# Turning the state with 64x64 products, and joining the inverse straight after X, in an RWKV-7 kernel with a GELU MLP

## The chip, the cores and the metric

The kernel runs on one core of a Trainium2 chip. The time is device time in microseconds of one execution. A core has five engines that run at the same time and each take their own instructions in order: TensorE (PE in the profile) multiplies matrices[...], ScalarE (ACT) evaluates functions and copies, VectorE (DVE) and GpSimd (POOL) work element by element, and SyncE (SP) issues most of the DMA transfers. An engine waits on semaphores until what it reads has been written and what it overwrites has been read.

## The reference

Inputs r, k, v, w, a, b have the shape (4 batches, 8 heads, 768 steps, 40). Each head keeps a 40x40 state:

```
y[t]   = r[t] . state
Sa     = state . a[t]
state  = state * w[t]  -  outer(Sa, b[t])  +  outer(v[t], k[t])
```

The y of all heads are put side by side to x (3072 x 320), and then

```
h = x @ w_in            # 320 x 2048
out = gelu(h) @ w_out   # 2048 x 320, exact (erf) GELU
```

## The kernel before

**Chunks.** The 768 steps are cut into 12 chunks of 64 steps. Inside a chunk the recurrence becomes matrix products; the state passes from chunk to chunk. Everything is float32. The 32 pairs of batch and head are laid in halves of 64 partitions: tiles are written [P, e, i, g, d] or the like, where e and x stand for halves, i counts pairs of heads, and g pairs of batches. Most products are therefore 64x64, 40x64 or 32x32 blocks, four or more of which have different places in TensorE's array (`mm`, line 100). `units` lists the 64 places (g, i, x, e).

**A turn of the loop** for chunk c (n = c+1, n2 = c+2 are the chunks that are prepared ahead) issues, in this order for TensorE: `corner` (J, 64 products of 32x32, and the copy Js on ScalarE), `make_X` (X, the state times a, summed with avs on VectorE), a piece of the MLP, `joined` (J again, 64 products of 32x32 from Js and the fetched T2 and Tt; then half of the result is copied to Tt by ScalarE and half by VectorE, line 723), a piece of the MLP, `make_sa` and `make_saT` from Tt and X, an MLP piece, `make_y2` (from the turned state) and `make_M`, an MLP piece, `make_QY`, `outputs` (y, and the new state, on VectorE), an MLP piece, `make_A(n)`, `sums(n2)`, `turn_state`, `make_av(n)`, an MLP piece, `make_RV(n)`, `make_N(n2)`, and two more MLP pieces. The order on each engine is the order in which the program issues (`manual_schedule`); there is no planner that moves it.

**The MLP** of a finished chunk is a generator of eight pieces; `fill()` runs the next one. Four pieces are `ph` (line 914, 40 products with w_in each, then Gelu on ScalarE, line 916), and from chunk 3 on the other four are `po` of `seven` (line 867, products with w_out in a scheme with seven products in place of eight; its sums on VectorE are lines 852, 871, 881, 887, 888 and 919). In `seven` the stores of the output are issued on SP; a `ph` piece issues no DMA.

**sums(n2)** makes the running products of the decays. TensorE writes the sums of log w to two PSUM tiles: wT_ps, turned, and cum, in rows. ScalarE then takes exponentials (line 436): wp = exp(+wT_ps), en = exp(-wT_ps), each in two instructions, one for each g, and rw = exp(-cum) (line 438; its tile is named part in the profile). wp scales a (`scale_a`, line 498, VectorE) and the new state, en scales the turned b and k (lines 507 and 525, VectorE), and rw scales the rows of b (`scale_b`, line 476, VectorE) and of k (`scale_k`, line 483, POOL).

**turn_state** transposes the state for `make_y2` of the next chunk: `flip` (line 446) makes eight 128x128 transposes on TensorE into the PSUM tile tn_ps, and ScalarE copies them to the tile turned (line 836).

**The inverse.** Each chunk needs the inverse of a triangular 64x64 matrix for each head. `make_N(n2)` makes N on TensorE, VectorE masks it (line 562), SP stores it to DRAM (line 599) and loads it as Nb in another layout (line 648). POOL inverts 32x32 blocks column by column (`start_inverse`, lines 656 and 658, 62 instructions with `scale_k` among them), and issues the store itself (line 670). In the next turn SP fetches the result as Tt and T2 (`fetch_inverse`, lines 680 and 684), VectorE turns a part of it to L (`turn_corner`, line 693), and `corner` and `joined` make the missing corner. So N made in turn c is needed by J at the start of turn c+2. SP issues its DMAs in program order: the fetch stands behind the transfers of xt (`outputs`, lines 815 and 818), and the store of the next N behind the fetch.

**PSUM** holds four tiles of two banks (`duo`); each new PSUM tile takes one of the four buffers once its last reader is done.

Ahead of the loop, chunks 0 and 1 are worked through by hand while the weights are loaded and converted; `turn_state` stands there twice.

Of the kernel before, what the change touches and what calls it, by code (L numbers as in the profile page):

```python
# [13 lines left out]
ACT = mybir.ActivationFunctionType  # L14
# [5 lines left out]
def kernel(  # L20
# [46 lines left out]
    nc = tc.nc  # L67
# [6 lines left out]
    NP = H // 2  # L74
    NA = H // 4
    G = B // 2
# [13 lines left out]
    def duo(name):  # L90
        return psum.tile([P, 2, 512], FP32, tag="duo", name=name)

    def half(j, n=HP):
        return slice(j * HP, j * HP + n)
# [4 lines left out]
    def mm(o, lhsT, rhs, first=True):  # L99
        nc.tensor.matmul(o, lhsT, rhs, start=first, stop=True, skip_group_check=True)  # L100
# [30 lines left out]
    NB = 4  # L131
# [77 lines left out]
    def load_v(c):  # L209
        if c >= NT:  # L210
            fetch_pairs(c, "v", v, nc.sync, True)
# [41 lines left out]
    ident = const.tile([P, P], FP32, name="ident")  # L253
# [30 lines left out]
    def flat(t):  # L284
        return t.rearrange("p j g n t -> p (j g n) t")
# [117 lines left out]
    def run(steps):  # L403
        for _ in steps:
            pass
# [8 lines left out]
    def sums(c):  # L414
        logw = raws.pop((c, "w"))
        pt = duo("wT_ps").rearrange("p e (n t) -> p e n t", t=C)
        for n in range(G * NP):
            for x in range(2):
                for e in range(2):
                    at = (2 * n + x) * D  # L420
                    mm(pt[half(x), e, n], logw[half(e), at:at + HP], cum_m[half(e), half(e)])
        cum = duo("cum")[:, :, :DM]
        for g in range(G):
            for e in range(1 if c < NB else 2):
                q = half(e ^ g) if c >= NB else slice(0, P)
                mm(cum[half(e) if c >= NB else q, g], cum_m[q, q], logw[q, g * DM:(g + 1) * DM])
        wp = wp_ring()
        turned_in.setdefault(c, {})["wp"] = wp
        if c < NB:
            nc.scalar.activation(wp[:, :, 1:].rearrange("p (n e) t -> p e n t", e=2), pt, ACT.Exp)  # L430
        else:
            en = turned_in.setdefault(c, {})["en"] = by_batch(side("en", "kT", 1))
            for to, scale_ in ((wp[:, :, 1:].rearrange("p (g n e) t -> p g e n t", g=G, e=2), 1.0),
                               (en.rearrange("p (e g n) t -> p g e n t", e=2, g=G), -1.0)):
                for g in range(G):
                    nc.scalar.activation(to[:, g], pt[:, ::1 - 2 * g, g * NP:(g + 1) * NP], ACT.Exp, scale=scale_)
        rw = (avs_ring if c in (1, 2) else part_ring)()[:, :, :DM]
        nc.scalar.activation(rw, cum, ACT.Exp, scale=-1.0)
        decays[c] = rw.rearrange("p g (h d) -> p g h d", h=H), wp

    def flip(src, name):

        pt = duo(name).rearrange("p g (n t) -> p g n t", n=NP)
        for g in range(G):
            for n in range(NP):
                nc.tensor.transpose(pt[:, g, n], src(g, n), ident)
        return pt
# [4 lines left out]
    def side(name, tag, bufs):  # L452
        return work.tile([P, G, NP, P], FP32, tag=tag, name=name, bufs=bufs)
# [4 lines left out]
    def by_batch(t):  # L458

        return t.rearrange("p g n t -> p (g n t)").rearrange("p (n t) -> p n t", t=C)  # L460
# [234 lines left out]
    def corner(c):  # L695

        t = turned_in[c]
        if "L" not in t:
            turn_corner(c)
        L = t.pop("L")  # L700
        N = flat(t["N"])
        J = duo("J")[:, 0].rearrange("p (n t) -> p n t", n=2 * G * NP)
        for n in range(2 * G * NP):
            for q in range(2):
                mm(J[(lo if n % 2 else hi)[q], n // 2], N[lo[q], n, BL:], L[lo[q], n])
        Js = work.tile([P, G * NP, BL], FP32, tag="Js", name="Js")
        nc.scalar.copy(Js, J[:, :G * NP])  # L707
        t["Js"] = Js

    def joined(c):  # L710
        t = turned_in[c]
        Tt, T2 = inverses.pop(c)
        Js = t.pop("Js")
        F = flat(Tt)
        J = duo("J2")[:, :, :G * NP * BL].rearrange("p z (n t) -> p z n t", n=G * NP)
        for n in range(2 * G * NP):
            for q in range(2):
                if n % 2:
                    mm(J[lo[q], 1, n // 2], Js[lo[q], n // 2], T2[lo[q], n // 2])
                else:  # L720
                    mm(J[lo[q], 0, n // 2], Js[hi[q], n // 2], F[hi[q], n, BL:])
        for q, copy in ((0, nc.scalar.copy), (1, nc.vector.tensor_copy)):
            copy(F[lo[q], :, BL:].rearrange("p (n z) t -> p z n t", z=2), J[lo[q]])  # L723
        t["Tt"] = Tt
# [4 lines left out]
    def make_X(c):  # L729
        t = turned_in[c]  # L730
        if state[0] is None:
            t["xs"] = t["avs"]
            return
        st = state[0][0]
        X = duo("X")[:, :, :G * NP * D].rearrange("p x (g i d) -> p x g i d", g=G, i=NP)
        for g, i, x, e, q, m in units():
            mm(X[half(e ^ x), x, g, i], t["aT"][half(x, D), g, i, e], st[half(x, D), e, i, g, :D])

        xs = t["xs"] = part_ring() if c == 1 else t["avs"]
        nc.vector.tensor_tensor(xs[:, :, :DM], X.rearrange("p x g i d -> p x (g i d)"), t["avs"][:, :, :DM], ALU.add)  # L740
# [92 lines left out]
    def turn_state():  # L833
        st = state[0][0]
        tn = side("turned", "turned", 1)
        nc.scalar.copy(tn, flip(lambda e, i: st[:, e, i].rearrange("p g d -> p (g d)"), "tn_ps"))
        state[0][1] = tn


# [105 lines left out]
    def fill(n=1):  # L945
        while n and pieces:
            if next(pieces[0], "end") == "end":
                pieces.pop(0)
            else:
                n -= 1  # L950
# [5 lines left out]
    def seconds(n, *loads, last=False):  # L956

        convert(n, last)
        for load in loads:
            second_load(*load)  # L960
# [9 lines left out]
    pt = duo("warm")  # L970
# [163 lines left out]
    for c in range(2, NCH):  # L1134
        n, n2 = c + 1, c + 2
        more, more2 = n < NCH, n2 < NCH
        corner(c)
        make_X(c)
        if c == NS + 1:
            weight_sums(3)  # L1140
        if c == 2:

            seconds(1, (14, 14), last=True)
            fill()
            turn_b(n)
            make_N(n)
            run(start_inverse(n, nc.gpsimd))
            store_inverse(n, (nc.gpsimd,))
            load_r(n)
            load_v(n)  # L1150
        else:
            fill()
        if more2:
            load_next(n2)
        joined(c)
        if c > 2 and more:
            scale_b(n)
        if c == 2:
            pieces.reverse()
            seconds(2, last=True)  # L1160
        fill()
        make_sa(c)
        make_saT(c)
        if c == 2:
            turn_r(n)
            scale_k(n, nc.vector)
            fill()
            pieces.reverse()
            fill(2)
            turn_k(n)  # L1170
        if more2:
            load_r(n2)
        if more2:
            turn_a(n2)
            fetch_pairs(n2, "b_turned", b, nc.sync, False, paired["a"])
        fill()
        make_y2(c)
        make_M(c)
        if more:
            turn_v(n)  # L1180
        if more2:
            load_v(n2)
            turn_r(n2)
            fetch_pairs(n2, "k_turned", k, nc.sync, False, paired["r"])
        fill()
        if more2:
            logs(n2)
        make_QY(c)
        outputs(c)
        pieces.append(mlp(c))  # L1190
        fill()
        if c == NS:
            weight_sums(0)
            weight_sums(1)
        if more:
            make_A(n)
        if more2:
            sums(n2)
        if more:
            turn_state()  # L1200
            fetch_inverse(n)
            make_av(n)
        if more2:
            scale_a(n2)
            turn_b(n2)
        fill()
        if c == NS:
            weight_sums(2)
        if more:
            make_RV(n)  # L1210
        if more2:
            make_N(n2)
            steps = start_inverse(n2, nc.gpsimd)
            load_kb(n2)
            load_VR(n2)
            for _ in range(BL // 4):
                next(steps)
            scale_k(n2)
            run(steps)
            store_inverse(n2, (nc.gpsimd,))  # L1220
        if more:
            turn_corner(n)
        fill()
        if more2:
            turn_k(n2)
        fill()
# [31 lines left out]
```

## Time and profile before

| | us |
|---|---|
| runs | 724.34, 724.49, 719.02 (median 724.34) |
| profiled execution | 717.79 |
| its span, first to last instruction | 716.1 |
| mean granted TensorE clock | 0.947 |
| busy TensorE / VectorE / ScalarE / POOL | 656.9 / 383.7 / 214.6 / 343.6 |
| start of J in c=2 to 11 | 157.36, 231.83, 284.68, 334.80, 384.94, 435.06, 485.88, 536.42, 586.55, 635.26 |
| start of POOL's inverse in c=3 to 10 | 232.97, 285.67, 338.04, 389.45, 439.40, 490.56, 541.65, 592.32 |

All times in the text are microseconds from the start of the span of the profiled execution, unless they are durations. A line of the order of time reads: start, duration, engine, line of the program, operation, output<-inputs, and a count where like instructions are merged; in brackets, how long the engine stood before it and what ended that. Matmuls are pipelined, so the duration of a group reaches past the start of the next one, and the distance from start to start is what the group takes of TensorE's time. A line of the waits reads: who waited for whom, the total, how often, the longest. A line of the chain reads: start, duration, what.

### The profile page before, as it was taken

Reading aid. Unit: us, or ns where it says so; the run is one execution under the profiler, and the core shown is the slowest. Engines: PE = TensorE matmul, PEld = TensorE weight load, DVE = VectorE, ACT = ScalarE, POOL = GpSimd, SP = SyncE. Lnnn points to the kernel's source line nnn. Section 1 sums busy time; section 2 is a strip of 40 time slices with the busy share of each in tenths; the row PEclk is TensorE's granted clock in tenths of the full one; section 3 lists DMA queues with packets and bytes.
Section 4 is the critical chain, followed back from the end, with each engine's and each line's share of the span. In section 5 each row is a group of like instructions: output and inputs, shape, how many; then the busy total and the mean of one; then the engine's idle time right before and its main releaser. Section 6 shows DMA issues by size and latency. Waiting matters only on the chain.

```text
span 716.1 us, 31454 instructions
## 1 busy us (share of the span) xinstructions
PE 656.9 (92%) x14128; PEld 575.5 (80%) x14128; DVE 383.7 (54%) x541; ACT 214.6 (30%) x295; POOL 343.6 (48%) x794
## 2 busy tenths in 40 slices
PE   7446789569999999999999999999999999999997
PEld 4345678557787877889899899998998998988987
DVE  2795579885245265366374483573672772521303
ACT  5115464343131341340351342232223413112020
POOL 4285248810670860871862853835836817800000
PEclk9655899678999999999999999999999999999999
DMA  9787749562764865765666757657747645020100
GB/s 121 131 164 152 137 101 232 120 112 56 146 134 87 134 122 88 123 122 92 127 118 116 132 99 127 125 95 128 141 73 140 132 91 77 21 54 4 28 12 19
DMA packets 284559, 75.76 MB, mean 106 GB/s; under 512 B 272232, under 2 KB 277128, under 8 KB 284424
## 3 DMA queue, kind: packets, MB, share of 16 engines
q1 hardware_dynamic: 283360, 71.22, 53.4%
q0 software_dynamic: 864, 2.36, 2.1%
q8 instruction: 111, 1.82, 1.1%
q14 instruction: 24, 0.20, 0.1%
q10 hardware_dynamic: 200, 0.16, 0.1%
HBM read 59.54 MB, written 10.22 MB: 97 GB/s over the span
## 4 chain that ended last, share of the span: by engine, by line
PE 49%; POOL 16%; DMA 11%; DVE 8%; SPq 7%; issue 5%; ACT 3%; ACTq 1%; POOLq 0%; DVEq 0%
PE ph L914 18%; PE po L931 8%; POOL W L658 8%; PE po L867 8%; POOL tmp L656 7%; PE QY L100 3%; DMA inv<-W 3%; DMA Nb<-N 2%; DMA N<-N 2%; PE J L100 2%; SPq L153 1%; DMA Tt<-inv 1%; DMA w_out_sb<-in_moe_w_in_dram 1%; DVE conv L314 1%; PE av L100 1%
## 5 line engine op out<-in xcount | busy, mean ns | idle before, releaser
L914 PE MATMUL ph<-xt,w_in_sb 64*128 64x256 f32 x1920 | 219.4, 381 | 1.3 <-ACT gt L916 1.1
L656 POOL TENSOR_TENSOR tmp<-W,Nb 128x126 f32<-128x126 f32 (+22 forms) x310 | 125.0, 403 | 164.4 <-DMA Nb<-N 141.5
L914 PEld LDWEIGHTS ph<-xt,w_in_sb 64*128 64x128 f32 x1920 | 182.2, 187 | 23.8 <-POOL W L646 0.8
L658 POOL TENSOR_TENSOR W<-W,tmp 128x126 f32<-128x126 f32 (+22 forms) x310 | 129.4, 418 | 24.3
L916 ACT ACTIVATE gt<-ph 128x1024 f32<-128x1024 f32 x48 | 49.1, 1023 | 148.8 <-PE ph L914 148.7
L867 PE MATMUL po<-w_out_sb,gt 128*128 128x160 f32 x576 | 82.9, 302 | 0.6 <-DVE gt L887 0.6
L867 PEld LDWEIGHTS po<-w_out_sb,gt 128*128 128x128 f32 x576 | 78.7, 190 | 2.7 <-DVE gt L887 0.9
L931 PE MATMUL po<-w_out_sb,gt 128*128 128x320 f32 x192 | 56.7, 453 | 0.0
L931 PEld LDWEIGHTS po<-w_out_sb,gt 128*128 128x128 f32 x192 | 37.4, 198 | 16.0 <-issue 2.3
L723 DVE COPY Tt<-J 32x512 f32<-32x512 f32 x12 | 8.3, 689 | 58.8 <-ACT Tt L723 58.7
L176 DVE STREAM_TRANSPOSE aT<-a_pairs 128x1024 f32<-128x1024 f32 x9 | 11.2, 1245 | 43.2 <-DMA a_pairs<-in_a_dram 43.2
L707 ACT COPY Js<-J 128x256 f32<-128x256 f32 x12 | 4.4, 370 | 99.2 <-PE J L100 99.2
L919 DVE TENSOR_TENSOR half<-gt 128x1024 f32<-128x1024 f32 x9 | 11.3, 1256 | 30.0 <-ACT gt L916 30.0
L310 ACT ACTIVATE conv<-conv,rebias 128x320 uint32<-128x320 uint32 (+1 forms) x26 | 16.0, 624 | 36.0 <-DVE conv L309 35.9
L867 PE MATMUL po<-extra,half 128*128 128x160 f32 x176 | 26.1, 303 | 0.0
L562 DVE TENSOR_TENSOR SM<-M_ps,upper 128x1024 f32<-128x1024 f32 x12 | 14.5, 1207 | 20.7 <-PE M_ps L100 20.7
L871 DVE TENSOR_TENSOR os<-os,po 128x160 f32<-128x160 f32 x36 | 11.5, 319 | 24.3 <-PE po L867 18.6
L867 PEld LDWEIGHTS po<-extra,half 128*128 128x128 f32 x176 | 24.2, 190 | 0.3
L916 ACT ACT_TABLE_LOAD x10 | 12.8, 1283 | 38.0 <-PE ph L914 38.0
L100 PE MATMUL av<-VR,A 64*64 64x40 f32 x768 | 15.7, 240 | 9.0 <-DVE A L562 7.3
L562 DVE TENSOR_TENSOR VR<-RV_ps,upper 128x1024 f32<-128x1024 f32 x12 | 14.7, 1223 | 16.6 <-PE RV_ps L100 16.6
L100 PEld LDWEIGHTS av<-VR,A 64*64 64x64 f32 x768 | 14.0, 149 | 11.3 <-DVE A L562 7.9
(199 smaller groups left out, 1109.4 us busy)
## 6 DMA issues: line engine op xcount, KB each, us to landing
Nb<-N SPq DMA_DIRECT2D x22, 256.0 KB
VR<-in_v_dram SPq DMA_DIRECT2D x24, 160.0 KB
out_dram<-os SPq DMA_DIRECT2D x48, 80.0 KB
b_rows<-in_b_dram SPq DMA_DIRECT2D x22, 160.0 KB
k_rows<-in_k_dram SPq DMA_DIRECT2D x22, 160.0 KB
w_out_sb<-in_moe_w_out_dram SPq DMA_DIRECT2D x11, 320.0 KB
N<-N SPq DMA_DIRECT2D x48, 64.0 KB
Tt<-inv SPq DMA_DIRECT2D x48, 64.0 KB
```

Of the source, the lines that this page charges most:

```text
L100: nc.tensor.matmul(o, lhsT, rhs, start=first, stop=True, skip_group_check=True)
L176: nc.vector.transpose(to.rearrange("p n (s y) -> p n y s", y=2), raws.pop((c, n)).rearrange("p n (y d) -> p n y d", y=2)[:, :, :, :BL])
L310: nc.scalar.activation(power, power, ACT.Relu, bias=rebias, scale=8.0)
L562: nc.vector.tensor_tensor(to, pt, upper.unsqueeze(1).to_broadcast([P, 2 * G * NP, C]), ALU.mult)
L656: eng.tensor_tensor(t, W[:, :rows, j:j + 1].to_broadcast([P, rows, rest]), Nb[:, j:j + 1, j + 1:].to_broadcast([P, rows, rest]), ALU.mult)
L658: eng.tensor_tensor(W[:, :rows, j + 1:], W[:, :rows, j + 1:], t, ALU.add)
L867: nc.tensor.matmul(po[:, n, :DM // 2], l_[:, f], r_[:, f], start=f == 0, stop=f == NF // 2 - 1)
L871: nc.vector.tensor_tensor(to, one_, other, ALU.add)
L914: nc.tensor.matmul(ph[:, x, s], w_in_sb[half(x), kt, p * P:(p + 1) * P], xt[half(x), kt], start=kt == 0, stop=kt == NK - 1)
L916: nc.scalar.activation(gt[:, 4 * q:4 * q + 4].rearrange("p (x s) t -> p x s t", x=2), ph, ACT.Gelu)
L919: nc.vector.tensor_tensor(s1, block(1, 0), block(1, 1), ALU.add)
L931: nc.tensor.matmul(po[:, g], gt[:, f, g * P:(g + 1) * P], w_out_sb[:, f], start=f == 0, stop=f == NF - 1)
```

## The change

Three things change. `turn_state` no longer calls `flip`: it makes 32 products of 64x64 blocks of the state with a 64x64 block of the identity, laid out by the half x that is read and the half g that is written, and the copy on ScalarE puts the halves in their places. In `sums`, from chunk 4 on, rw is made after wp and ahead of en. In the loop, from c=3 on, `joined(c)` stands directly behind `make_X(c)` (and the sums of the weights, in c=4), ahead of the MLP piece and of `load_next(n2)`, instead of behind them.

```diff
@@ sums
         else:
             en = turned_in.setdefault(c, {})["en"] = by_batch(side("en", "kT", 1))
-            for to, scale_ in ((wp[:, :, 1:].rearrange("p (g n e) t -> p g e n t", g=G, e=2), 1.0),
-                               (en.rearrange("p (e g n) t -> p g e n t", e=2, g=G), -1.0)):
-                for g in range(G):
-                    nc.scalar.activation(to[:, g], pt[:, ::1 - 2 * g, g * NP:(g + 1) * NP], ACT.Exp, scale=scale_)
+            for g in range(G):
+                nc.scalar.activation(wp[:, :, 1:].rearrange("p (g n e) t -> p g e n t", g=G, e=2)[:, g],
+                                     pt[:, ::1 - 2 * g, g * NP:(g + 1) * NP], ACT.Exp)
         rw = (avs_ring if c in (1, 2) else part_ring)()[:, :, :DM]
         nc.scalar.activation(rw, cum, ACT.Exp, scale=-1.0)
+        if c >= NB:
+            for g in range(G):
+                nc.scalar.activation(en.rearrange("p (e g n) t -> p g e n t", e=2, g=G)[:, g],
+                                     pt[:, ::1 - 2 * g, g * NP:(g + 1) * NP], ACT.Exp, scale=-1.0)
@@ turn_state
         tn = side("turned", "turned", 1)
-        nc.scalar.copy(tn, flip(lambda e, i: st[:, e, i].rearrange("p g d -> p (g d)"), "tn_ps"))
+        pt = duo("tn_ps").rearrange("p x (e i t) -> p x e i t", e=2, i=NP)
+        for e in range(2):
+            for i in range(NP):
+                for g in range(G):
+                    for x in range(2):
+                        mm(pt[half(g), x, e, i], st[half(x), e, i, g], ident[half(x), half(x)])
+        nc.scalar.copy(tn.rearrange("p e i (x t) -> p x (e i) t", x=2), pt.rearrange("p x e i t -> p x (e i) t"))
@@ the loop
         else:
+            joined(c)
             fill()
         if more2:
             load_next(n2)
-        joined(c)
+        if c == 2:
+            joined(c)
```

## The prediction

> **What bounds the kernel now.** I read the busy times by engine first, then the waits of TensorE, then one turn of the loop in order of time, and last the chain that ended last.
>
> ```profile
> PE 656.9 (92%) x14128; PEld 575.5 (80%) x14128; DVE 383.7 (54%) x541; ACT 214.6 (30%) x295; POOL 343.6 (48%) x794
> ```
>
> TensorE is the fullest engine; asked by stretches, it is busy for 50.12 of 50.12 us in the turns c=4 and c=6. What shortens its queue in the loop therefore counts, until something else is late. The waits of TensorE (total, times, longest) name what could be late:
>
> ```profile
> PE J L100 <- DVE L L693: 11.0, 4, 5.8
> PE av L100 <- DVE A L562: 7.3, 3, 5.7
> ...
> PE av L100 <- ACT en L436: 1.1, 2, 0.6
> ```
>
> TensorE's order of time around turn_state in c=4 (start, us, instruction, count) and ScalarE's beside it:
>
> ```profile
> 317.84 1.11 PE L100 MATMUL wT_ps<-cum_m,w_tile 64*64 64x64 f32 x64
> 318.77 0.72 PE L100 MATMUL cum<-w_tile,cum_m 64*64 64x320 f32 x8
> 319.42 1.09 PE L446 MATMUL tn_ps<-ident,st 128*128 128x128 f32 x8
> 320.44 1.14 PE L100 MATMUL av<-VR,A 64*64 64x40 f32 x64
> 321.51 0.68 PE L867 MATMUL po<-extra,half 128*128 128x160 f32 x3
> ```
> ```profile
> 319.02 1.09 ACT L436 ACTIVATE wpT<-wT_ps 128x512 f32<-128x512 f32 x2 [0.27 <-PE wT_ps L100]
> 320.00 1.08 ACT L436 ACTIVATE en<-wT_ps 128x512 f32<-128x512 f32 x2
> 320.94 0.74 ACT L438 ACTIVATE part<-cum 128x640 f32<-128x640 f32 x1
> ```
>
> From start to start, the eight transposes hold TensorE for 320.44-319.42 = 1.02 us, and 64 products of 64x64 hold it for 318.77-317.84 = 0.93 us. Last the end of the chain, before the last corner:
>
> ```profile
> 622.53 1.17 POOL W L658
> 625.95 0.81 POOL inv L670
> 626.76 4.40 DMA inv<-W
> 631.59 2.71 DMA Tt<-inv
> 634.40 0.72 DVE L L693
> ```
>
> From about 412 to 636 us the chain isn't TensorE's: it runs round inverse on POOL, store, fetch on SP, store of the next N on SP, Nb, next inverse. This ring turns in about 51 us (POOL starts 389.45, 439.40, 490.56, 541.65, 592.32) against TensorE's 50.1, so L comes ever closer to J: ready at 330.26 for a J at 334.80 (c=5), at 584.04 for 586.55 (c=10), and in c=11 TensorE waits 0.54 us for it. **Two bounds thus lie side by side**, and a gain on TensorE alone is lost at the last corner.
>
> [...] J2 between two MLP pieces takes 341.84-341.16 = 0.68 us, as J does elsewhere. [...] a W step of POOL that normally takes 0.38 us took 0.95 at 546.49, while scale_b ran on VectorE from 546.37. [...]
>
> **The change, part by part.** Times are those of the profiled execution: its span is 716.1, its own time 717.79, and the median of the runs is 724.34, 6.55 more, which I can't place.
>
> *The turn of the state.* Eight transposes go, 32 products of 64x64 come. They have wT_ps's form and order (four tiles in turn), so 32/64 x 0.93 = 0.47 us: 0.55 saved a turn. The copy that follows still moves 1024 elements, now written in runs of 64: 1.06 us as before. Bounds: 0.47 if only the product is cheaper, up to 1.02 if full-array work between 64x64 work had a hidden price.
> - c=4 to 9, six turns: av may start 0.55 sooner, for its mask on A ends at 319.31 and av would come at 319.89. Saved: 6 x 0.55 = 3.3 us.
> - c=2 and 3: av waited for en (0.6 and 0.45 us); see the next part. c=10: av already waits 0.32 for A, so nothing. The two turns ahead of the loop: behind the second, J waits 5.8 us for L; nothing.
>
> *The order on ScalarE.* Nothing is added; rw (0.74 us) goes ahead of en. cum's PSUM buffer is free 0.94 us sooner and wT_ps's 0.65 later. In the program of before, buffers are taken in the order of their release: after av in c≥4, po gets wT_ps's, RV_ps cum's, N_ps tn_ps's. With rw first I take it that po gets cum's: rw ends at 320.00+0.74 = 320.74 and po would come at 321.51-0.55 = 320.96, 0.2 us of cover. In c=2 and 3 av gets it in place of wT_ps's: rw would end at 267.12+0.74 = 267.86 (c=3), 0.35 before en did, so 0.35 us each, 0.7 in all. Behind en wait turned and avs on ScalarE, but the three together take as long as before; nT's scaling, which needs en, starts at 323.02 and en is now done at 321.73. POOL's scale_k reads rw some 25 us later: nothing.
>
> *The join.* Its 64 products move ahead of an MLP piece, with no change in number: 0. New is that only X (1.07 us) covers the copy Js: J ends at 335.55, Js at 336.16, X at 336.57, so 0.4 us of cover; without it the join would stall TensorE by up to 0.6. The fetched T2 has landed before, L being made of the same fetch. The first piece's Gelu comes 0.7 later; its buffer is wanted a piece or more later. No DMA is issued in joined or in an MLP piece of `ph`, so **SP and POOL keep their order**. On VectorE, the copy to Tt stood 6.5 us waiting with scale_b behind it. Now the copy follows the sum of X, and scale_b runs about 4.1 us after J starts instead of 9.9 (J 536.42, scale_b 546.37).
>
> *What that does to the ring.* The N made in turn c=4 is stored as soon as its mask ends (329.64, store 329.67), so the ring starts sooner by the lead that TensorE has there: 0.7+0.55 = 1.25 us. Later stores follow the fetch, so the lead is carried along. From c=6 on POOL's inverse starts 4.3 to 5.8 us after J, and with TensorE further ahead 5.0 or more (c=6: 389.45-1.25 against 384.94-1.8). scale_b now ends at 4.1+0.8 = 4.9, before that, in c=6 to 10, and POOL is spared the excess of one step each: 0.47, 0.57, 0.48, 0.57, 0.47, together 2.56. L of c=11 comes 1.25+2.56 = 3.81 us sooner. Bounds: 1.25 if scale_b's leaving changes nothing; and if POOL, now later against VectorE's work, meets one more two-input operation (0.86 us each, as beside L881) in three turns, 1.25-2.58 = -1.33.
>
> *Sum.* TensorE is ready for the last corner 0.7+3.3 = 4.0 us sooner, plus the 0.54 that it idled there. L comes 3.81 sooner: that is later than TensorE's 4.54, so it decides, and after it everything is TensorE's and unchanged. 717.79-3.81 = 714.0 for the profiled execution; **724.34-3.81 = 720.5 for the median**, -0.5%.
>
> **Rivals.**
> - *The ring keeps the gain.* scale_b leaves but POOL meets other operations instead: gain 1.25, or 723.1. For it: in c=9 and 10 POOL's steps already meet L498, L887 and L888 (0.87 to 0.96 each). Against it: in c=6 and 7 only scale_b, L919 and L881 are met. At its worst bound 725.7.
> - *Slower: po still gets wT_ps's buffer.* Then po waits for en's end at 321.73 plus 0.05, 0.27 later than before, six times, and av in c=2 and 3 waits 0.6 longer: 1.6+1.2 = 2.8 us, less the 0.5 that TensorE idled at the last corner: +2.3, 726.6. It decides as soon as the buffer comes more than 0.2 us after rw. For it: that buffer is po's now. Against: release order explains the buffers of every turn that I followed.
> - *More than forecast.* Runs 6 us longer than the profiled one may hold a late ring in every turn. POOL would then start later after J, and scale_b would leave all eight of its windows, not five: 2.56 and the excess in c=3 to 5 (0.62, 0.50, 0.59) make 4.27, with the 1.25 in front 5.5: 718.8. Against it: this profile shows the wait in one turn alone.
> - *It does nothing:* if the products of 64x64 with the identity cost what the transposes did, only the ring's 2.56 is left, and TensorE is late: 724.34-0.7-0.54 = 723.1.
>
> **How the numbers follow.** Forecast 0.5; the ring keeps it 0.18; po waits 0.1; more than forecast 0.15; nothing 0.07. The runs of before spread over 5.5 us, so 1% (7.2 us) is about what can be told from no change. Faster by over 1% (below 717.1) takes a median among the short executions, with either of the larger gains (719.02-3.81 = 715.2): 0.20. Slower by over 1% (beyond 731.6) takes the waiting po together with a ring that slips further: 0.03. The rest, 0.77, is within 1%. The range goes from 714.0 (the short executions) to 726 (the ring's worst bound, and most of the waiting po).
>
> **What would show it.** tn_ps near 0.47 us from start to start; av and po following with no wait; joined right behind X, with no wait for Js; scale_b before POOL's first W step from c=6 on, and POOL's inverses 0.5 us shorter; J of c=11 near 631.5, still waiting a little for L. The forecast is wrong if po waits for en, if Js holds up the join, or if L of c=11 doesn't come sooner.

## The result, and the profile after

The changed kernel takes **741.19 us** in the median (740.9 to 748.76) against 724.32 for the kernel before. The ratio of the means is 1.0276, 95% interval 1.0225 to 1.0327. It is slower, where 720.5 was forecast. Here and below a ratio is that of the means, with executions over 1.5% above the fastest of their kernel left out, while medians and ranges are those of all. The profiled execution of after has a span of 739.2 us at a mean granted clock of 0.939 (before 716.1 and 0.947). Of the 23.1 us between the spans 2.2 lie ahead of J in c=3 (234.04 against 231.83), 21.1 between J of c=3 and J of c=11 (424.56 against 403.43; "the loop" below), and -0.2 behind that. The first part differs by more than that between executions of programs that are the same up to there (231.83 before, 236.94 in the run with scale_b moved), so only the loop is followed.

The busy times by engine, after:

```profile
PE 663.4 (90%) x14744; PEld 583.3 (79%) x14744; DVE 381.8 (52%) x541; ACT 216.0 (29%) x295; POOL 336.2 (45%) x794
```

There are 616 more matmuls (14,128 before), 56 for each of 11 turns of the state. The forecast had 24 more, 32 in place of eight. And TensorE's share fell to 90%, though the kernel is longer: it now stands still. What for is in the waits of TensorE (who waited for whom, total, times, longest):

```profile
PE J L100 <- issue: 8.2, 3, 3.3
...
PE av L100 <- issue: 4.5, 5, 1.4
...
PE ph L923 <- issue: 2.1, 2, 1.2
PE tn_ps L100 <- issue: 2.1, 3, 0.9
...
PE po L876 <- issue: 1.4, 1, 1.4
```

"issue" names no engine and no DMA: nothing that the profile records as a wait had to end. Between J of c=3 and J of c=11 TensorE is idle for 17.4 us, against 2.0 before. The order of time on TensorE around the turn of the state in c=4 (start, duration, instruction, count; in brackets the idle time before it), and on ScalarE:

```profile
323.93 1.11 PE L100 MATMUL wT_ps<-cum_m,w_tile 64*64 64x64 f32 x64
324.87 0.72 PE L100 MATMUL cum<-w_tile,cum_m 64*64 64x320 f32 x8
325.41 1.11 PE L100 MATMUL tn_ps<-ident,st 64*64 64x64 f32 x64
326.34 0.61 PE L100 MATMUL av<-VR,A 64*64 64x40 f32 x27
327.82 0.78 PE L100 MATMUL av<-VR,A 64*64 64x40 f32 x37 [0.88 <-issue]
```
```profile
325.12 1.09 ACT L434 ACTIVATE wpT<-wT_ps 128x512 f32<-128x512 f32 x2 [0.27 <-PE wT_ps L100]
326.09 0.71 ACT L437 ACTIVATE part<-cum 128x640 f32<-128x640 f32 x1
326.67 1.11 ACT L440 ACTIVATE en<-wT_ps 128x512 f32<-128x512 f32 x2
```

Here is the miscount: the 32 products of the turn stand as x64. Every fp32 product of `mm` is two matmul instructions in the trace, and wT_ps, which also stands as x64, is made by 32 of them; a transpose is one (x8 before). So the turn takes 326.34-325.41 = 0.93 us, 0.09 less than the transposes and not 0.55. What stands beside it gains too: cum in front takes 325.41-324.87 = 0.54, where it took 0.65 ahead of the transposes, and av behind it 1.02 where nothing stops it (c=9), for 1.07. Together a turn saves 0.25 us. ScalarE's order went as forecast. And in the middle of av, with 27 of its matmuls done, TensorE stops for 0.88 us.

The join of c=6, in the order of time on TensorE and on ScalarE:

```profile
392.86 0.83 PE L100 MATMUL J<-L,N 32*32 32x32 f32 x64
393.62 1.14 PE L100 MATMUL X<-st,aT 40*64 40x40 f32 x64
394.69 0.22 PE L100 MATMUL J<-Tt,Js 32*32 32x32 f32 x2
...
395.07 0.19 PE L100 MATMUL J<-Tt,Js 32*32 32x32 f32 x1
397.67 0.20 PE L100 MATMUL J<-Tt,Js 32*32 32x32 f32 x1 [2.41 <-issue]
...
398.13 11.19 PE L923 MATMUL ph<-xt,w_in_sb 64*128 64x256 f32 x80
```
```profile
393.81 0.37 ACT L710 COPY Js<-J 128x256 f32<-128x256 f32 x1 [9.29 <-PE J L100]
```

The join starts right behind X, and Js, done at 394.18, doesn't hold it. It runs for half a microsecond and then stops in its middle for 2.41. After that two MLP pieces take 409.25-398.13 = 11.1 us, where two take 9.0 before. The stretches around it (length, busy time of each engine with its instructions, granted TensorE clock, DMA share, GB/s) say why:

```profile
390.00:395.20 5.20, 5.20 (x192) 4.89 (x191) 4.19 (x8) 0.37 (x1) 0.00 (x0) 1.00 0.67 136
395.20:397.70 2.50, 0.09 (x11) 0.03 (x5) 0.45 (x1) 0.00 (x0) 1.21 (x5) 0.66 0.88 104
397.70:401.00 3.30, 3.30 (x36) 2.71 (x37) 1.51 (x2) 0.57 (x1) 2.75 (x8) 0.50 1.02 180
401.00:405.00 4.00, 4.00 (x32) 3.40 (x30) 0.00 (x0) 0.00 (x0) 3.61 (x8) 0.77 0.58 121
405.00:410.00 5.00, 5.00 (x94) 4.21 (x90) 0.00 (x0) 2.87 (x3) 4.22 (x11) 1.00 0.94 166
```

The stop costs a second time: the clock falls to half (0.50 from 396.0 to 402.8), here while TensorE still stands (0.66 in the stretch of the stop), and is at half for 5.1 us behind it. That happens at each of the three stops in the join (c=3, 6, 10; 2.49, 2.41 and 3.33 us), and the two pieces that follow take 10.4, 11.1 and 11.0 us, 5.4 us over 9.0 each in all. The idle time grew by 17.4-2.0 = 15.4; with the 5.4 that is 20.8. The cheaper turn gives 6 x 0.25 = 1.5 back in c=4 to 9, which leaves 19.3 of the 21.1 us. The rest, 1.8, isn't split further. It may lie in the stops, which cost more than their idle time: the av of c=4 takes 2.19 us with a stop of 0.88, which is 0.29 more than 1.02 and the stop together.

The chain that ended last, as shares by engine, before and after:

```profile
PE 49%; POOL 16%; DMA 11%; DVE 8%; SPq 7%; issue 5%; ACT 3%; ACTq 1%; POOLq 0%; DVEq 0%
```
```profile
PE 78%; DVE 7%; issue 4%; SPq 3%; POOL 2%; DMA 2%; ACT 2%; ACTq 1%; DVEq 0%; POOLq 0%
```

The ring round POOL, on which the forecast's sum was made, has left the chain: L of c=11 ends at 653.86, for a J at 658.60.

**Where the stops lie.** The DMA queues of the page have one that brings instructions (packets, MB, share of 16 engines), in after:

```profile
q8 instruction: 116, 1.90, 1.1%
```

Its packets are of 16,384 bytes, and 2 x 14,744 matmuls and weight loads make 254 for each of the 116. I read the start and end of its packets from the DMA records, and counted matmuls and weight loads (n) from the start of the program up to the instruction at which TensorE stops. These are seven of the twelve stops in the loop of after:

```
after          packet starts  ends    TensorE stops  goes on   n
c=3, join      235.75  237.25         236.18         238.67     8075
c=4, av        325.26  326.57         326.95         327.82    12151
c=5, av        376.66  377.94         378.28         379.33    14697
c=6, join      395.13  396.36         395.26         397.67    15461
c=7, tn_ps     431.02  432.30         433.05         433.86    16989
c=9, av        535.71  537.11         537.12         538.50    22083
c=10, join     606.54  608.02         606.26         609.59    25393
```

Each stop ends 1.25 to 1.6 us after a packet's end, or 2.5 to 3.05 after its start. And the counts differ by whole packets: 12151-8075 = 16 x 254.75, 14697-12151 = 10 x 254.6, 15461-14697 = 3 x 254.7, and so on to 25393, 68 packets of 254.68 from the first (a packet may hold some instructions that these records leave out). **TensorE stops where one packet of instructions ends and the next hasn't come.** How long a packet takes comes out of the stops too: the loops of the thirteen profiles have 62 of over 0.15 us put to "issue", all of them lie at whole packets of the count (to 0.11 of a packet), and each ends 2.2 to 3.3 us after its packet's start, 1.2 to 1.9 after its end.

A packet's 254.7 instructions last about 1.8 us as small products (14.5 ns for a matmul with its load beside it), and some 14.4 as an MLP piece (40 matmuls of `ph` with their loads in 4.52 us, 286.43 to 290.95 in the kernel before). By this count, the next packet starts between 1.5 us before and 1.9 us after the first instruction of most blocks in the loop of after, and 1.9 to 2.4 after it for some blocks that begin in J or X (3.1 once, behind the stop in c=6). So a block made of small products alone runs out, if its successor's packet hasn't started early. The change has longer unbroken runs of them: J, X and the join are 192 products' pairs of load and matmul (128 for J and X before), and A_ps to av are 264 (208 before).

### The profile page after: what moved, and what is told of

It is laid out like the page before. It is cut to its first block, busy times and chain, and to the rows that moved or that the text cites. A ratio compares the mean times of both kernels' runs of the same rounds, so it can differ in the third digit from the quotient of the medians.

```text
span 739.2 us, 32661 instructions
## 1 busy us (share of the span) xinstructions
PE 663.4 (90%) x14744; PEld 583.3 (79%) x14744; DVE 381.8 (52%) x541; ACT 216.0 (29%) x295; POOL 336.2 (45%) x794
## 4 chain that ended last, share of the span: by engine, by line
PE 78%; DVE 7%; issue 4%; SPq 3%; POOL 2%; DMA 2%; ACT 2%; ACTq 1%; DVEq 0%; POOLq 0%
PE ph L923 27%; PE po L876 18%; PE po L940 8%; PE QY L100 5%; PE J L100 2%; PE X L100 2%; PE RV_ps L100 2%; PE av L100 2%; PE wT_ps L100 2%; PE A_ps L100 2%; PE tn_ps L100 1%; PE N_ps L100 1%; PE sap L100 1%; PE M_ps L100 1%; POOL st L661 1%
## 5 line engine op out<-in xcount | busy, mean ns | idle before, releaser
L923 PE MATMUL ph<-xt,w_in_sb 64*128 64x256 f32 x1920 | 223.5, 387 | 3.3 <-issue 2.1
L923 PEld LDWEIGHTS ph<-xt,w_in_sb 64*128 64x128 f32 x1920 | 187.0, 191 | 28.3 <-issue 3.0
L659 POOL TENSOR_TENSOR tmp<-W,Nb 128x126 f32<-128x126 f32 (+22 forms) x310 | 119.4, 385 | 183.9 <-DMA Nb<-N 160.9
L754 DVE COPY SM<-sap 128x640 f32<-128x640 f32 x12 | 9.9, 823 | 65.9 <-PE sap L100 65.8
```

The lines of the kernel that those rows point to most:

```text
L659: eng.tensor_tensor(t, W[:, :rows, j:j + 1].to_broadcast([P, rows, rest]), Nb[:, j:j + 1, j + 1:].to_broadcast([P, rows, rest]), ALU.mult)
L923: nc.tensor.matmul(ph[:, x, s], w_in_sb[half(x), kt, p * P:(p + 1) * P], xt[half(x), kt], start=kt == 0, stop=kt == NK - 1)
```

## The experiments

Theory A: TensorE outruns its instruction packets in runs of small products that the change made longer. Rivals: the turn in 64x64 tiles costs by itself; the join waits for Js or for the fetched blocks; scale_b and ScalarE's order disturb something. Times are medians with their range, ratios are to the kernel before beside them with the 95% interval; loops are those of the profiled executions (403.43 before).

### Each part alone

**The turn alone** (`turn_state` of the change in the kernel before):

```diff
-        nc.scalar.copy(tn, flip(lambda e, i: st[:, e, i].rearrange("p g d -> p (g d)"), "tn_ps"))
+        pt = duo("tn_ps").rearrange("p x (e i t) -> p x e i t", e=2, i=NP)
...
+                        mm(pt[half(g), x, e, i], st[half(x), e, i, g], ident[half(x), half(x)])
```

> The kernel before with the turn by 64x64 products alone. Theory A (instruction supply): each of the 32 products is two matmul instructions, so 64 take the place of 8, TensorE saves only 1.02-0.93 = 0.1 us a turn, and the run of small instructions A_ps, wT_ps, cum, tn_ps, av grows from 208 to 264 pairs; TensorE then runs dry for 0.8 to 1.4 us inside tn_ps or av in most turns, right behind the start of an instruction packet: 728 to 732 us. Theory B (the loss is all in the join): within 1.5 us of before, no stall inside tn_ps or av. Theory C (the number of TensorE instructions counts, wherever they stand): all of the loss, 738 to 742.

Measured: 728.54 us (725.78 to 733.04), 1.0085 (1.0058 to 1.0113). The loop is 7.9 us longer, with 9.7 us of idle time: one stop of 0.7 to 1.6 us in tn_ps or av in each of the turns c=3 to 10, no half clock. The time is as expected under A. Its waits of TensorE:

```profile
PE av L100 <- issue: 5.7, 6, 1.4
PE tn_ps L100 <- issue: 3.4, 3, 1.6
```

**The join alone** (the loop of the change in the kernel before; no instruction is added or left out):

```diff
         else:
+            joined(c)
             fill()
...
-        joined(c)
+        if c == 2:
+            joined(c)
```

> The kernel before with joined directly behind X alone; no instruction is added. Theory A: J, X and the join make one run of 192 pairs in place of 128 and 64, and TensorE runs dry for 2.4 to 3.3 us inside the join in some turns, with a stretch of half clock behind each: 732 to 738 us. Theory B' (the join waits for the copy Js): up to 0.6 us at the first product of the join in each of nine turns, no half clock: 724 to 730. Theory C: no change.

Measured: 743.69 us (740.44 to 748.24), 1.0266 (1.0188 to 1.0344); loop +21.4. That is more than the 732 to 738 expected. The matmuls are the same 14,128, so what costs is their order. There are stops of 2.1 to 3.5 us in the join, half clock with those of the loop, and two stops in `ph`:

```profile
PE J L100 <- issue: 11.5, 4, 3.4
PE ph L914 <- issue: 3.2, 2, 2.2
```

They lie in c=3, 5 and 8, and after the loop in c=11, where after's lay in c=3, 6 and 10. The two loops don't add up: 7.9 and 21.4 us alone, 21.1 together. Each part moves the places at which packets end. The medians alone wouldn't show it, since the interval of the join alone is 1.6% wide.

**rw ahead of en alone:**

```diff
-            for to, scale_ in ((wp[:, :, 1:].rearrange("p (g n e) t -> p g e n t", g=G, e=2), 1.0),
-                               (en.rearrange("p (e g n) t -> p g e n t", e=2, g=G), -1.0)):
...
         nc.scalar.activation(rw, cum, ACT.Exp, scale=-1.0)
+        if c >= NB:
+            for g in range(G):
+                nc.scalar.activation(en.rearrange("p (e g n) t -> p g e n t", e=2, g=G)[:, g],
+                                     pt[:, ::1 - 2 * g, g * NP:(g + 1) * NP], ACT.Exp, scale=-1.0)
```

> The kernel before with rw ahead of en alone. All theories: no TensorE instruction is touched; av of c=2 and 3 starts about 0.3 us sooner each, po takes cum's buffer without a wait: 723 to 724.5 us. If po had to wait for en it would be 727.

Measured: 722.59 us (715.54 to 731.86), 0.9986 (0.9954 to 1.0017): no change that can be told. In the profile av waits 0.23 us in c=2 in place of 0.61 and 0.10 in c=3 in place of 0.45, together the 0.7 that was forecast. The loop, which has only c=3 in it, is 402.69, 0.74 shorter; that is near 0.7 by chance, for J of c=11 doesn't wait in this execution, which gives 0.54 of it.

**scale_b moved alone**, the join staying where it was:

```diff
         else:
+            if more:
+                scale_b(n)
             fill()
...
         joined(c)
-        if c > 2 and more:
-            scale_b(n)
```

> The kernel before with scale_b issued ahead of the join, so that it runs right behind the sum of X; nothing on TensorE moves. The forecast's ring step: scale_b leaves POOL's window from c=5 on, POOL's inverses there are 0.5 us shorter, L of c=11 comes some 2.5 us sooner, and J of c=11 no longer waits its 0.5 us: 717.3 in the profiled execution, 720 to 724 for the median (the lower end if the ring is what makes the longer executions longer). If the step is wrong: no change, and POOL's windows are as long as before.

Measured: 722.7 us (716.84 to 727.3), 0.9992 (0.9962 to 1.0023), loop 403.23. scale_b didn't leave POOL's inverses: in c=6 to 10 it still starts 2.0 to 2.8 us after they do, and the last one lasts 33.30 us against 33.32. That of c=8 is 0.9 us shorter, but it is so with rw alone too (31.23 here, 31.19 there, 32.16 before), where scale_b wasn't moved. VectorE's order of time shows why:

```profile
497.49 0.82 DVE L476 SCALAR_TENSOR_TENSOR b_rows<-b_rows,part 128x640 f32<-128x640 f32 x1 [3.23 <-DMA b_rows<-in_b_dram]
```

It waits for the rows of b to be loaded. From c=5 on it runs 5.8 to 8.2 us after J starts (here 497.49-491.54), not 4.1.

### The same work with the runs broken up

**The join directly behind X, but an MLP piece between J and X:**

```diff
         corner(c)
+        if c > 2:
+            fill()
         make_X(c)
...
         else:
-            fill()
+            joined(c)
...
-        joined(c)
+        if c == 2:
+            joined(c)
```

> The kernel before with the join directly behind X as in the change, but with the MLP piece between the corner and X: J, piece, X, join, piece. The join has no piece in front, the longest run of small products there is 128 pairs again. Theory A (instruction supply): the stalls of 2 to 3 us in the join are gone, 721 to 724.5 us. Rival D (what hurts is the join right behind X: its data, its PSUM buffer or the change of tiling from 64x64 to 32x32 without a piece between): as slow as the join alone, 740 to 744.

Measured: 722.8 us (716.0 to 728.33), 0.9991 (0.9946 to 1.0036), loop 403.14. No stop in the join and no half clock in the loop; TensorE's order of time in c=6:

```profile
383.92 0.75 PE L100 MATMUL J<-L,N 32*32 32x32 f32 x64
384.60 4.59 PE L914 MATMUL ph<-xt,w_in_sb 64*128 64x256 f32 x40
389.12 1.14 PE L100 MATMUL X<-st,aT 40*64 40x40 f32 x64
390.19 0.22 PE L100 MATMUL J<-Tt,Js 32*32 32x32 f32 x2
...
390.87 1.35 PE L914 MATMUL ph<-xt,w_in_sb 64*128 64x256 f32 x10
```

The join follows X as in the change, with Js long done, and costs nothing. This alone would also fit a wait for Js; that is parted further on.

**The turn between the last two MLP pieces** of the loop, away from other small products:

```diff
-            turn_state()
             fetch_inverse(n)
...
+        if more:
+            turn_state()
         fill()
```

> The kernel before with the turn by 64x64 products as in the change, but issued between the last two MLP pieces of the turn instead of ahead of av. Same number of instructions as the turn alone, which was 0.85% slower. Theory A: no stall inside tn_ps or av, 0.1 us a turn saved: 721 to 724 us. Theory C (the number of instructions counts) or products of 64x64 that are slow in themselves: 727 to 730, as the turn alone.

Measured: 725.46 us (722.5 to 729.57), 1.0107 (1.0069 to 1.0145). The stops in tn_ps are gone, as A says, but the expected time is missed: the loop of the profile is 406.30, 2.9 longer than before, where the turn alone was 7.9 longer, and the ratio is no better than that of the turn alone (1.0085). So the profiles show what became of the stops; that it saves time isn't shown.

```profile
532.67 4.61 PE L873 MATMUL po<-w_out_sb,gt 128*128 128x160 f32 x32
537.21 1.16 PE L100 MATMUL tn_ps<-ident,st 64*64 64x64 f32 x64
538.30 2.44 PE L873 MATMUL po<-extra,gt 128*128 128x160 f32 x16
540.67 0.75 PE L100 MATMUL J<-L,N 32*32 32x32 f32 x64
```

The turn takes 538.30-537.21 = 1.09 us here, and the 16 po behind it 2.37 where 32 in front take 4.54. Together that is 1.19, 0.26 more than between small products and 0.17 more than the transposes took: 1.4 us in eight turns. Part of the rest is av, which with no turn in front waits 1.35 us for the mask of A in c=10 (0.32 before), and stops for 0.31, 0.35 and 0.72 in c=3, 6 and 7.

### More small products, that wait for nothing

**32 more products of 32x32 directly behind X**, from N and L, which J has read before; nothing reads their result and nothing is left out:

```diff
         make_X(c)
+        if c > 2:
+            extra_products(c)
```

> The kernel before with 32 more products of 32x32 (those of the corner again, into a PSUM tile that nobody reads) directly behind X, from c=3 on; the join stays where it was. They cost 0.68 us in each of nine turns, 6.1 us, by themselves. Theory A: the run J, X, more is 192 pairs, as in the join alone, and nothing in it waits for Js, Tt or T2: stalls of 2 to 3 us and half clock behind them all the same, 736 to 750 us. Rival D: 727.5 to 730, the price of the products alone.

Measured: 753.5 us (749.73 to 755.33), 1.0466 (1.0408 to 1.0525), above even the 736 to 750 of A. The loop is 27.4 us longer, of which the products are 8 x 0.68 = 5.4. TensorE's order of time in c=5:

```profile
341.14 0.75 PE L100 MATMUL J<-L,N 32*32 32x32 f32 x64
341.83 1.14 PE L100 MATMUL X<-st,aT 40*64 40x40 f32 x64
342.90 0.45 PE L100 MATMUL more<-L,N 32*32 32x32 f32 x30
345.97 0.74 PE L100 MATMUL more<-L,N 32*32 32x32 f32 x34 [2.62 <-issue]
```

The run J, X, more has the same 192 pairs as J, X, join in the change, and stops in its middle in the same way, though it needs no Js and no fetched block. The wait for Js is out.

**The same products behind the join of the kernel before**, with an MLP piece between them and X:

```diff
         joined(c)
...
+        if c > 2:
+            extra_products(c)
         fill()
```

> The same 32 more products, directly behind the join, between two MLP pieces: a run of 128 pairs. Theory A: 727.5 to 730 us, the price of the products alone. Theory C (number of instructions): as slow as with the products behind X.

Measured: 734.08 us (729.79 to 735.38), 1.0193 (1.0135 to 1.0251), loop +13.8. For the same added work that is half the cost, so the place matters, but it is more than expected: eight stops of 0.2 to 1.5 us remain, and the longest, in c=5, brings half clock, which costs the piece behind it 1.7 us. Runs of 128 pairs with one MLP piece between them can still run dry; what I took for a safe length isn't one.

### The place of the packets

**The changed kernel, with 32 products ahead of the loop**, where TensorE waits for L in any case:

```diff
     turn_state()
+    pt = duo("shift")
+    for n in range(16):
+        for q in range(2):
+            mm(pt[half(q), q, n * BL:(n + 1) * BL], ident[half(q), half(q)], ident[half(q), q * HP:q * HP + BL])
     seconds(3)
```

> The changed kernel, with 32 extra products of 64x32 (64 matmul instructions and their weight loads, half of what one instruction packet brings) put ahead of the loop, behind the second turn_state, where TensorE waits 5.8 us for L of c=2 anyway; nothing reads their result and nothing is left out. They move every later instruction of TensorE by half a packet and change nothing in the loop. Theory A (TensorE runs out of delivered instructions, and where depends on how the packets fall on the program): the long stalls of 2.4 to 3.3 us leave the joins of c=3, 6 and 10 for other turns or for ph pieces, with a total of 10 to 25 us of idle time between J of c=3 and c=11, and 735 to 750 us. Rival (the stalls belong to what those turns do, or wait for data of those turns): stalls in the joins of c=3, 6 and 10 again, at the same 2.4, 2.4 and 3.3 us.

Measured, in two executions: 745.08 us (742.04 to 748.12), 1.0348 (1.0212 to 1.0485). The loop has not one instruction more than that of after, takes 424.43 us against 424.56, and has 17.0 us of idle time against 17.4. But the stops have moved: 2.67 in the join of c=4 and 3.00 in that of c=8, none in those of c=3, 6 and 10. Two of them in TensorE's order of time:

```profile
296.12 0.18 PE L100 MATMUL J<-T,Js 32*32 32x32 f32 x1 [2.67 <-issue]
...
331.21 0.74 PE L100 MATMUL tn_ps<-ident,st 64*64 64x64 f32 x35 [0.46 <-issue]
```

By the count of matmuls and weight loads from the program's start they lie where after's lay, and in the program 128 of these earlier:

```
n         after                     with 32 products ahead of the loop
12151     in av, 327.82             in tn_ps, 331.21
14697     in av, 379.33             in tn_ps, 385.48
22083     in av, 538.50             in tn_ps, 546.02
24629     in po behind av, 590.97   in av, 599.65
```

The others lie at other whole packets of the same count. Nothing that these instructions read or write has this property. That shows the packet's end to be the cause of the stops.

**The turn by 16 products of 64x128**, one for both g, in the kernel before: half the instructions of the change's turn.

```diff
-                for g in range(G):
-                    for x in range(2):
-                        mm(pt[half(g), x, e, i], st[half(x), e, i, g], ident[half(x), half(x)])
+                for x in range(2):
+                    mm(pt[:, x, e, i], st[half(x), e, i].rearrange("p g d -> p (g d)"), ident[half(x), half(x)])
```

> The kernel before, with the turn of the state made by 16 products of 64 rows and 128 columns of weights in place of the change's 32 products of 64x64, at the same place: the same result. Two of them lie side by side in the array instead of four, so I expect the same 0.93 us, but 32 instruction pairs in place of 64; the run of small products from A_ps to av has 232 pairs (208 before, 264 with the turn of 64x64 alone, which stalled 9.7 us in the loop). Theory A (instruction supply): stalls between those of the two, 2 to 6 us in the loop, and 723 to 727 us. Rival (work in 64x64 tiles there is what costs, and not the number of instructions): the stalls of the 64x64 turn vanish altogether or stay as they are, with 722 or 728.

Measured: 730.02 us (725.46 to 732.11), 1.0132 (1.0029 to 1.0235), outside both expectations. The stops are gone (0.13 us of idle time in the loop), but the products take twice the time that I took them to:

```profile
326.10 2.00 PE L100 MATMUL tn_ps<-ident,st 64*128 64x64 f32 x32
328.04 1.14 PE L100 MATMUL av<-VR,A 64*64 64x40 f32 x64
```

32 matmuls take 1.94 us, 61 ns each, where those of 64x64 take 14.5. The loop is 5.05 us longer. So this run doesn't measure how the stops go with the number of instructions, since the slow turn (1.94 us in place of 0.93) also gives the packets time. It does show that work in tiles of 64 rows in place of 128 brought no stop by itself.

**The two harmless parts together** (rw ahead of en, and J, piece, X, join, piece):

```diff
         nc.scalar.activation(rw, cum, ACT.Exp, scale=-1.0)
+        if c >= NB:
...
         corner(c)
+        if c > 2:
+            fill()
         make_X(c)
...
         else:
-            fill()
+            joined(c)
```

> The kernel before, with rw made ahead of en, and with the order J, MLP piece, X, join, MLP piece in place of J, X, piece, join, piece: the two parts of the change that cost nothing, with no run of small products made longer. The two loops alone were 0.74 and 0.29 us shorter than before. Theory A: no stall in the join, loop 1.0 us shorter, 721.5 to 722.5 for a kernel before of 722.5, which can't be told from no change. Rival (the join directly behind X costs by itself): a stall in the join in some turns, 725 or more.

Measured: 720.5 us (718.25 to 728.33), 1.0001 (0.996 to 1.0042). No gain and no loss that can be told. The loop of its profile is 405.83, not the expected 402.4: c=9 has stops of 0.45 us in ph and 0.65 in saT_ps, a packet apart, which the same order of TensorE's instructions in the earlier run with the spread join didn't have. The joins have none.

## Why the prediction was wrong

*The turn of the state.* "32 products ... 32/64 x 0.93 = 0.47 us" failed. The x64 of wT_ps are matmul instructions, and the program makes 32 products there, so the row had the price of exactly this turn: 0.93. The count was at hand, in the program beside the trace. The saving, forecast as 0.55 a turn, was 0.09 in the turn's own row and 0.25 with cum and av beside it. The 0.16 in the neighbours is the "hidden price" of full-array work that the upper bound allowed for. J2 and J, 0.68 us each, couldn't show it, since both stand behind MLP pieces; what makes the price isn't shown. The same miscount is in other places ahead of the result: J and the join are 32 products each and not 64, a `ph` piece is 20 and not 40. There it changes no sum, since their times were read from the trace.

*The resource that no step had.* Every step priced time on an engine, a wait or a buffer; that TensorE's instructions have to be delivered was in none, so no rival could reach 741. The part that was put at "no change in number: 0", the join, is the one that costs most: alone it takes 21.4 us in the loop with not one instruction more. The chances for slower by over 1% (0.03) rested on a waiting po alone. The profile before had the queue of instructions on its page and waits for "issue" in its list, of 0.3 to 0.7 us; the one in its loop, 0.48 us in av of c=7, ends 2.57 us after a packet's start like those of after. Together with the run of 192 pairs, which the change makes in 2.5 us, they would have raised the question, though not the amount, as none of these waits was long.

*The join.* "0.4 us of cover" for Js was right, and so was the claim that SP and POOL keep their order. With the spread join the step is worth nothing, as forecast for the join on TensorE. "scale_b runs about 4.1 us after J" was wrong by another term: the rows of b arrive later (with scale_b moved alone it runs 5.8 to 8.2 us after J from c=5 on).

*The ring.* Its 3.81 us were to come from scale_b leaving POOL's inverses, 2.56, and from the lead, 1.25. With scale_b moved alone it stays inside the inverses, and none of these is shorter by the forecast 0.5 us that isn't so without the move; so that 2.56 falls, for a reason apart from the packets. In after it can't be judged, as TensorE is far behind the ring.

*The order on ScalarE.* Right: in the run with rw alone av's waits in c=2 and 3 fell by 0.38 and 0.35 us, 0.7 in all as forecast, and po waits for nothing: in c=4 it starts at 325.80, before en ends at 325.87. No median can show that.

*The rivals.* None came. po never waited for en. The premise of the last one, that the products cost what the transposes did, was nearly so (0.93 for 1.02), but its 723.1 had no stops in it.

**What stays open:** why the next packet starts 0.5 us after a block's first instruction in one place and 1.9 to 2.4 in another. Hence which short blocks stop can't be told from their length: in after, a block of 1.75 us in the join of c=5 doesn't stop, and that of c=9 pauses for 0.2 us (554.27 to 554.48), since their successor's packet had started 1.2 and 0.6 us ahead of their first instruction. The stops aren't the same in every execution either: the run with rw alone has TensorE's order of before and stops for 2.86 us at 82.7, ahead of the loop, where before has no such stop. Whether other DMA traffic delays the packets wasn't tested. And some 3.0 us of the loop with the products behind the join (13.8, less 5.4 of products, 3.6 of idle time and 1.7 of half clock), and 1.7 of that with the two harmless parts, have no place that I could show.

## What to carry to other kernels

Count TensorE's instructions as the trace does, not the program's products (here two for an fp32 product, one for a transpose), and price their packets like any other transfer: here a packet's 254.7 instructions lasted about 1.8 us as small products, and the packets behind the stops took 2.2 to 3.3 us from their start to their first instruction. Taking a large piece out from between two such runs, which looks free, cost this kernel 2.7% (1.9 to 3.4) in the run with the join alone. Look for "issue" in TensorE's waits and for the instruction queue on the page before lengthening a run of small products, and try large products between them: with a piece between J and X the join had no stop (0.9991, 0.9946 to 1.0036). What parted the packet's end from a wait of the kernel's own was a shift of the program by 128 instructions: the stops stayed at counts such as 12151 and 14697, 128 instructions earlier in the program.

## What the hardware showed that I had not expected

- TensorE's instructions come in packets of 16,384 bytes, about 254.7 recorded matmuls and weight loads each. From a packet's start to its first instruction 2.2 to 3.3 us passed at the stops; in none of the thirteen profiles do two packets start closer than 3.29 us between 160 and 690 us.
- The clock went to half in or behind stops of 2.41 to 3.33 us, for 3.4 or 6.8 us (in after 3.4 from 239.0, 6.8 from 396.0 and 6.8 from 607.6). In c=6 the clock falls 0.7 us after TensorE stopped (395.26), behind 2.4 us of small products; in c=10 it falls 1.3 us after (606.26), in c=3 2.8 us after (236.18). In the run with the products behind the join a stop of 1.53 us among 32x32 products was enough, and in that with 32 products ahead of the loop one of 1.76 us in `ph` wasn't, so the length of the stop alone doesn't decide; what does isn't shown.
- The same turn in 64x64 tiles costs 0.93 us between other 64x64 work and 1.19 between full-array pieces, what the next piece loses counted in; and eight full-array transposes between 64x64 products make these 0.16 us longer (0.11 in cum, 0.05 in av).
- Two tiles of 64 rows that use all 128 columns gave 61 ns a matmul, against 14.5 for four tiles of 64x64.
